# Chunk 4's norm, transposes, Q, K and V worked in a gate-up stage; the first down stage in another order; exponential, value loads and the last down weights issued at other points

## The chip, the core and the metric

One core of a Trainium2 chip. The metric is the device time of one execution in microseconds (us). Engines are called PE (matrix), DVE (vector), ACT (scalar), POOL and SP; here the last two mostly issue transfers. Each engine works through its own instructions strictly in the order in which they stand in the program.

## What is computed

One transformer block with conditioning (adaptive layer norm) over 2048 rows of 576 values, in bfloat16: sliding local attention, then a gated product as feed-forward part.

```
mod = silu(c) @ w_mod  ->  sa, ca, ga, sb, cb, gb          (576 each)
h = layernorm(x) * (1 + ca) + sa
q, k, v = h @ wqkv                                         (32 heads of 18)
logits[s, w] = q[s] . k[s - 2w] * scale, w = 0..7          (8 keys, every second row back)
x = x + ga * (softmax(logits) @ v) @ wo
h = layernorm(x) * (1 + cb) + sb
x = x + gb * ((h @ w_gate) * (h @ w_up)) @ w_down          (576 -> 4608 -> 576)
```

## The kernel before

**Chunks and stages.** The rows are cut into eight chunks of 256 for the attention, and into five groups (line 43) for the feed-forward part: row tiles of 128, (0,2), (2,6), (6,10), (10,13), (13,16). For each group there is a gate-up stage (`gate_up`, line 734: 36 column blocks f of 128) and a down stage (`down`, line 790: the same 36 blocks as depth). They are called G0, D0, G1, D1, up to G4, D4 here. What comes ahead of G0 handles chunk 0 and the projections of chunks 1 and 2.

**Attention beside it.** The attention of the other chunks is cut into pieces, closures in lists with a guessed cost each, and `spread` (line 724) hands them out over the 36 blocks by the sum of costs. A list for gate-up stages is in `gbg` (line 1118), one for down stages in `dbg` (line 1139). Since every engine keeps program order, a piece on PE that waits holds back all the matmuls behind it, those of the feed-forward part too.

**One chunk's way.** `a_ln`, `a_norm` (338, 343): statistics and norm on DVE, with Ln and Exp on ACT (`rsq`, 258) between the two. `a_t` (358): T, ten transposes on PE into `hT`, evicted by DVE (line 286) or ACT (line 288). `a_q` (387): Q and K in five groups (line 377). `a_v` (395): V, written to DRAM (`vd`, line 411). `b_p` (421): eight products prod = q times shifted k on DVE (line 425). `b_lq` (429): twice 20 matmuls that sum them by head (`lg`, 435). `b_lt` (445): transposes of the logits (`lt`). `b_sm0` (454): maximum, difference, Exp on ACT (464). `b_sm1` (467): sums and quotient on DVE. `b_ld` (413): shifted values from DRAM into `vsh`, 1152 KB for each 128 rows, issued by POOL. `b_mul`, `b_add` (481, 487): values times weights, summed on DVE (485, 492, 494, 496) into `o_sb`. `b_o` (498): transposes of `o_sb` (line 505). `b_w` (649): output projection (`pw`, 658) and its eviction on DVE (660, 661). `b_ln`, `b_norm`, `b_t`: second norm and its transposes into `h2T`, which the next gate-up stage reads.

**Pairs.** Depth 576 is four and a half times 128. In the gate-up stages two matmuls of 64 rows each run side by side in the two halves of the array (`half`, line 513). `pair_unit` (526) does the same for Q, K and V of a chunk: units between the blocks of a gate-up stage, nine half steps for a pair of products in place of ten. Before, chunks 5, 6 and 7 (`PAIRED`, line 42) are done so in G1, G2 and G3; chunks 3 and 4 are projected in D0 with five depth steps each, the fifth half empty. `load_pair_rows` (519), the last piece of D0, loads what the pairs need in the upper 64 rows.

**D0 before.** The list is `gb_row` (1132: the row gb, ten matmuls; it also issues load 2 of the down weights, whose buffer it has just read), then chunk 1's output mixed with chunk 3's projections and 14 DVE pieces `b_mul`/`b_add` of chunk 2 (lines 1122 to 1130), then chunk 2's output mixed with chunk 4's norm, T, Q, K and V.

**Loads.** Gate and up weights (`load_wgu`, 145) are issued by SP, one block for four f, three buffers. Down weights (`load_wd`, 160) are issued by POOL, one block of 576 KB for four f, three buffers: block n + 3 is issued when block n has been used. Value loads of chunk 7 (`values(7)`) are issued both at once in G3.

Of the kernel before, what the change touches and what calls it, by code (L numbers as in the profile page):

```python
# [38 lines left out]

MODK = (0, 4, 1, 2, 3)  # L40
QKK = (0, 1, 4, 2, 3)
PAIRED = (5, 6, 7)
GROUPS = [(0, 2), (2, 6), (6, 10), (10, 13), (13, 16)]


# [1 line left out]
def kernel(  # L47
# [84 lines left out]
    def load_x(i):  # L132
        if i < NCH:
            x_in[i] = sp.tile([P, ST, D], BF, name="x_t1") if i == 1 else xin.tile([P, ST, D], BF, name="x_t")
            nc.sync.dma_start(x_in[i][:], x_rows(i))
# [22 lines left out]
            nc.sync.dma_start(wgr[64 * t:64 * (t + 1), cs], wsrc[KF * P:D, cs])  # L158

    def load_wd(g):  # L160
        if g >= NG * NBLK:
            return
        r0 = (g % NBLK) * FB * P
        wb = wdp.tile([P, FB, D], BF, name="wd")
        wd_blk[g] = wb
        return nc.gpsimd.dma_start(wb[:], B_w_down[r0:r0 + FB * P, :].rearrange("(k p) n -> p k n", p=P))  # L166

    def load_k(dst, wsrc, c0, n):
        r = nc.sync.dma_start(dst(slice(0, P), slice(0, KF)), wsrc[0:KF * P, c0:c0 + n].rearrange("(k p) n -> p k n", p=P))
# [168 lines left out]
    def a_ln(i):  # L338
        x = x_in.pop(i)
        xn, rsq, norm = layernorm(lambda j: x[:, j, :], "a")  # L340
        aa[i] = dict(xn=xn, rsq=rsq, norm=norm)

    def a_norm(i):
        aa[i]["rsq"]()
        aa[i]["norm"]()
# [12 lines left out]
    def a_t(i, on_dve=(0, 1, 2), between=None):  # L358
        a_tiles(i)
        hT = aa[i]["hT"]  # L360
        transposed(aa[i]["xn"], lambda m: hT[:, m, :], (0, 1), 0, between, KT if i in PAIRED else KF)(on_dve)

# [24 lines left out]
    def a_q(i, g):  # L387
        qk_tiles(i, QGRP[g], slice(0, CH), nc.scalar.copy)
        if g == 2:
            a_halo(i)  # L390
# [22 lines left out]
    def b_ld(i, j):  # L413
        b = bb.setdefault(i, dict(prod={}, vsh={}))
        base = HALO + i * CH + j * P - DIL * (W - 1)
        vsh = vshp.tile([P, W, DH, H], BF, name="vsh")
        vsrc = bass.AP(vd.tensor, vd.offset + base * D, [[D, P], [DIL * D, W], [1, D]])
        b["vsh"][j] = vsh
        return nc.gpsimd.dma_start(vsh[:].rearrange("p w d h -> p w (d h)"), vsrc)  # L419
# [9 lines left out]
    def b_lq(i, wq):  # L429
        b = bb[i]  # L430
        if wq == 0:
            b["lg"] = ps([P, 2, CH], F32, "lg")
        for m in range(KT):
            for wl in range(4):
                nc.tensor.matmul(b["lg"][H * wl:H * (wl + 1), wq, :], lhsT=ind[:, m, :], rhs=b["prod"][4 * wq + wl][:, m, :],  # L435
                                 start=(m == 0), stop=(m == KT - 1), skip_group_check=True)
        for wl in range(4):
            b["prod"].pop(4 * wq + wl)
        if wq == 1:
            lgs = lgp.tile([P, 2, CH], BF, name="lgs")  # L440
            nc.scalar.copy(lgs[:], b.pop("lg")[:])
            b["lgt"] = lgp.tile([P, 2, ST, 4, H], BF, name="lgt")
            b["lgs"] = lgs

    def b_lt(i):
        b = bb[i]
        lgs = b.pop("lgs")
        pt = ps([P, 2, ST, P], BF, "lt")
        for a in range(2):
            for j in range(ST):  # L450
                nc.tensor.transpose(pt[:, a, j, :], lgs[:, a, js(j)], ident[:])
        nc.scalar.copy(b["lgt"][:].rearrange("p a j w h -> p (a j w h)"), pt[:].rearrange("p a j n -> p (a j n)"))

    def b_sm0(i):
        b = bb[i]
        lg = b.pop("lgt")
        mx = smp.tile([P, ST, 4, H], BF, name="mx", tag="tree")
        dd = smp.tile([P, 2, ST, 4, H], F32, name="dd")
        nc.vector.tensor_tensor(mx[:], lg[:, 0], lg[:, 1], ALU.max)
        nc.vector.tensor_tensor(mx[:, :, 0:2], mx[:, :, 0:2], mx[:, :, 2:4], ALU.max)  # L460
        nc.vector.tensor_tensor(mx[:, :, 0], mx[:, :, 0], mx[:, :, 1], ALU.max)
        for wq in range(2):
            nc.vector.tensor_tensor(dd[:, wq], lg[:, wq], mx[:, :, 0:1].to_broadcast([P, ST, 4, H]), ALU.subtract)
        nc.scalar.activation(dd[:], dd[:], ACTF.Exp, scale=scale)
        b["dd"] = dd

    def b_sm1(i):
        b = bb[i]
        dd = b.pop("dd")
        ss = smp.tile([P, ST, 4, H], F32, name="ss", tag="tree")  # L470
        nc.vector.tensor_tensor(ss[:], dd[:, 0], dd[:, 1], ALU.add)
        nc.vector.tensor_tensor(ss[:, :, 0:2], ss[:, :, 0:2], ss[:, :, 2:4], ALU.add)
        nc.vector.tensor_tensor(ss[:, :, 0], ss[:, :, 0], ss[:, :, 1], ALU.add)
        rs = smp.tile([P, ST, 1, H], F32, name="rs")
        nc.vector.reciprocal(rs[:, :, 0], ss[:, :, 0])
        attn = attnp.tile([P, 2, ST, 4, H], BF, name="attn")
        for wq in range(2):
            nc.vector.tensor_tensor(attn[:, wq], dd[:, wq], rs[:].to_broadcast([P, ST, 4, H]), ALU.mult)
        b["attn"] = attn
# [188 lines left out]
    def b_norm(i):  # L668
        bb[i]["rsq"]()
        bb[i]["norm"]()  # L670
# [12 lines left out]
    def B_pr(i, w0, w1):  # L683
        return [(0.83, lambda w=w: b_p(i, w)) for w in range(w0, w1)]

    def B_lq(i, wq):
        return [(0.0, lambda: b_lq(i, wq))]

    def B_sm(i, turned=None):
        return [(0.5, lambda: b_lt(i))] + ([(1.0, lambda: a_t(turned))] if turned else []) + [ (1.2, lambda: b_sm0(i)), (0.6, nop), (1.8, lambda: b_sm1(i))]  # L690

    def B_wait(us):
        return [(us, nop)]

    def B_two(a, b, av_a, av_b, turned=None):
        return (B_pr(a, 0, 6) + B_lq(a, 0) + B_pr(a, 6, 8) + B_pr(b, 0, 2) + B_lq(a, 1) + B_pr(b, 2, 6) + B_lq(b, 0) + B_sm(a)
                + B_pr(b, 6, 8) + av_a[:4] + B_lq(b, 1) + av_a[4:] + B_sm(b, turned) + av_b)

    def B_one(a, ld, av_a):
        return B_pr(a, 0, 4) + ld + B_pr(a, 4, 6) + B_lq(a, 0) + B_pr(a, 6, 8) + B_wait(1.5) + B_lq(a, 1) + B_wait(4.0) + B_sm(a) + av_a  # L700

    def B_av(i):
        r = []
        for j in range(ST):
            r += [(0.7, lambda j=j, w=w: b_mul(i, j, w)) for w in range(0, W, 2)]
            r += [(0.7, lambda j=j: b_add(i, j, 0)), (0.7, lambda j=j: b_add(i, j, 1)), (1.2, lambda j=j: b_add(i, j, 2))]
            if i in (3, 5):
                r.append((0.0, lambda j=j: b_ld(i + 1, j)))
        return r

    def out_qkv(i, n):
        o = [lambda: b_o(i), lambda: b_w(i, 0), lambda: b_w(i, 1), lambda: b_ln(i), lambda: b_norm(i), lambda: b_t(i, (0,) if i == 6 else (0, 1))]
        if n >= NCH or n == 5 and n in PAIRED:
            return [o[0], nop, o[1], o[2], o[3], o[4], nop, o[5]]
        if n in PAIRED:
            return [lambda: a_ln(n), o[0], lambda: (a_norm(n), load_x(n + 2)), o[1], lambda: a_t(n), o[2], o[3], nop, o[4], nop, nop, o[5]]
        q, v = [lambda g=g: a_q(n, g) for g in range(5)], [lambda j=j: a_v(n, j) for j in range(ST)]
        return ([lambda: a_ln(n), o[0], lambda: (a_norm(n), load_x(n + 2))] + [nop] * (3 if n == 4 else 0) + [o[1], lambda: a_t(n), o[2], o[3]] + q[:1] + [o[4]] + q[1:]
                + [o[5]] + v)

    def nop():
# [390 lines left out]
    def res(i):  # L1112
        return (0.0, lambda: load_res(i))

    def values(i):
        return [(0.0, lambda: [b_ld(i, j) for j in range(ST)])]

    gbg = {0: B_two(1, 2, B_av(1) + [res(2), (0.0, load_wm5), (0.0, lambda: load_wd(0))], []),
           1: values(3) + B_two(3, 4, B_av(3) + [res(3), res(4), (2.4, lambda: a_ln(5)), (1.2, lambda: (a_norm(5), load_x(7)))], B_av(4), 5),
           2: values(5) + B_two(5, 6, B_av(5) + [res(5), res(6)], B_av(6)),  # L1120
           3: B_one(7, values(7), B_av(7)) + [res(7)]}
    av2 = [p for _, p in B_av(2)]
    oq = out_qkv(1, 3)
    first = []
    while oq or av2:
        if oq:
            first.append(oq.pop(0))
        if len(first) > 3:
            first += [p for p in av2[:2]]
            del av2[:2]  # L1130

    def gb_row():
        mod_row(lambda p, k: wm5[p, k, :] if k < KF else wm5r[p, :], gb_bc, sc_bc2)()
# [2 lines left out]
        b_ld(2, 1)  # L1136
        load_wd(2)

    dbg = {0: [gb_row] + first + out_qkv(2, 4) + [load_pair_rows],
           1: out_qkv(3, 5) + out_qkv(4, 6),  # L1140
           2: out_qkv(5, 7) + out_qkv(6, 8),
           3: [nop, lambda: b_t(6, (1,))] + out_qkv(7, 8)}
    units = {1: qkv_units(5, [(29, 0, 1), (30, 1, 2), (31, 2, 3), (32, 3, 4), (33, 4, 5)]),
             2: qkv_units(6, [(0, 0, 1), (1, 1, 2), (2, 2, 3), (3, 3, 4), (4, 4, 5)]),
             3: qkv_units(7, [(0, 0, 3), (1, 3, 4), (2, 4, 5)])}
    for gi in range(NG):
# [37 lines left out]
```

## Time and profile before

| | |
|---|---|
| time, three runs | 559.43, 559.93, 561.68 us (median 559.93) |
| profiled execution | 559.92 us, its span 558.2 us |
| busy: PE, weight loads, DVE, ACT, POOL | 548.4, 323.7, 330.1, 251.3, 63.2 us |
| granted PE clock | 1.00 |
| starts of G0, D0, G1, D1 | 49.62, 89.56, 133.28, 214.57 us |
| starts of G3, G4, D4 | 381.24, 474.03, 526.78 us |

A time-line row gives the start and the length in us, engine, line, operation, output and inputs, the shapes, and how many equal instructions it sums up; square brackets hold the idle time ahead of it and what ended it. Matmuls overlap, so their cost is read from one start to the next, not from their length. In a table of windows each row is a stretch of time: its length, the busy time (and number of instructions) of each engine, the granted clock, the share of the DMA engines in use and GB/s.

### The profile page before, as it was taken

The numbers are of one execution on the slowest core, as the hardware profiler recorded it, in microseconds if no ns is written. First come the engines' busy times: TensorE is split into PE (matmuls) and PEld (weight loads), VectorE is DVE, ScalarE is ACT, GpSimd is POOL, SyncE is SP. The second block draws the span as 40 slices with busy tenths as digits, with TensorE's granted clock in tenths as the row PEclk, the third lists the DMA queues.
The fourth block names the chain that finished last, engine by engine and source line by source line (L and its number), as shares of the span: only waits on it lengthen the run. The fifth ranks groups of instructions, "written<-read, shape, count | busy, mean of one in ns | idle before, by whom it ended". The sixth has DMA issues, their size and how long they took to land.

```text
span 558.2 us, 14633 instructions
## 1 busy us (share of the span) xinstructions
PE 548.4 (98%) x6195; PEld 323.7 (58%) x6195; DVE 330.1 (59%) x796; ACT 251.3 (45%) x592; POOL 63.2 (11%) x98
## 2 busy tenths in 40 slices
PE   8999999999999999999999999999999999999996
PEld 4887796665444465555544445556656555555564
DVE  7888798985777763546468686445527615322202
ACT  2746666344555663212655553114556511565500
POOL 3102101123001001112000000111200022000020
PEclk9999999999999999999999999999999999999999
DMA  8999999645647744336624955444685665565063
GB/s 263 281 272 322 345 296 354 213 151 185 236 142 241 229 143 140 109 105 208 229 80 155 300 172 156 128 125 132 201 266 180 207 180 193 167 210 162 2 177 109
DMA packets 70155, 108.38 MB, mean 194 GB/s; under 512 B 3690, under 2 KB 57850, under 8 KB 70090
## 3 DMA queue, kind: packets, MB, share of 16 engines
q1 hardware_dynamic: 58832, 61.50, 35.9%
q0 software_dynamic: 11168, 45.81, 25.6%
q8 instruction: 48, 0.79, 0.6%
q14 instruction: 17, 0.14, 0.1%
q10 hardware_dynamic: 90, 0.15, 0.1%
HBM read 103.00 MB, written 4.44 MB: 192 GB/s over the span
## 4 chain that ended last, share of the span: by engine, by line
PE 56%; issue 27%; DMA 4%; POOL 2%; DVE 1%; ACT 0%; POOLq 0%; SPq 0%; ACTq 0%
PE pg L513 16%; PE acc L803 13%; PE pu L513 13%; PE pp L513 4%; DMA wd<-in_B_w_down_dram 2%; PE pw L658 2%; PE accr L807 2%; POOL wd L166 2%; PE pq L377 2%; DMA wgu<-in_B_w_up_dram 2%; PE lg L435 1%; PE pv L400 1%; PE tr_pA L299 1%; POOL vsh L419 1%; PE oT_pA L505 0%
## 5 line engine op out<-in xcount | busy, mean ns | idle before, releaser
L513 PE MATMUL pg<-h2T,wgu 64*128 64x512 bf16 (+2 forms) x1440 | 279.7, 333 | 0.0
L513 PE MATMUL pu<-h2T,wgu 64*128 64x512 bf16 (+2 forms) x1440 | 277.9, 333 | 0.7 <-DMA wgu<-in_B_w_up_dram 0.7
L513 PEld LDWEIGHTS <-wgu 64*128 64x128 bf16 x2880 | 141.5, 94 | 105.4 <-DMA wgu<-in_B_w_up_dram 1.1
L761 ACT CAST u_sb<-pu 128x512 bf16<-128x512 f32 (+2 forms) x180 | 90.1, 501 | 132.6 <-PE pg L513 128.9
L803 PE MATMUL acc<-wd,hh 128*128 128x512 bf16 (+1 forms) x588 | 142.7, 370 | 0.5 <-DMA wd<-in_B_w_down_dram 0.4
L767 DVE TENSOR_TENSOR hh<-g_sb,u_sb 128x512 bf16<-128x512 bf16 (+2 forms) x180 | 66.8, 372 | 109.6 <-ACT g_sb L762 108.2
L807 PE MATMUL accr<-wd,hh 128*128 128x64 bf16 x576 | 99.4, 193 | 0.7 <-DMA wd<-in_B_w_down_dram 0.7
L762 ACT CAST g_sb<-pg 128x512 bf16<-128x512 f32 (+2 forms) x180 | 91.4, 508 | 0.0
L803 PEld LDWEIGHTS <-hh 128*128 128x128 bf16 x588 | 55.2, 98 | 59.6 <-issue 1.7
L166 POOL DMA_DIRECT2D wd<-in_B_w_down_dram x45 | 33.9, 753 | 255.5 <-PE accr L807 238.3
L513 PE MATMUL pu<-h2T,wgr 64*128 64x512 bf16 (+2 forms) x180 | 60.3, 335 | 0.3 <-ACT u_sb L761 0.3
L513 PE MATMUL pg<-h2T,wgr 64*128 64x512 bf16 (+2 forms) x180 | 60.3, 335 | 0.2 <-DVE h2T L286 0.2
L807 PEld LDWEIGHTS <-hh 128*128 128x128 bf16 x576 | 51.8, 98 | 3.2 <-issue 1.6
L425 DVE TENSOR_TENSOR prod<-qT,kT 128x1280 bf16<-128x1280 bf16 x56 | 44.7, 819 | 8.5 <-ACT kT L356 4.3
L485 DVE TENSOR_TENSOR vsh<-vsh,attn 128x1152 bf16<-128x1152 bf16 x56 | 40.9, 752 | 0.0
L513 PEld LDWEIGHTS <-wgr 64*128 64x128 bf16 x360 | 18.1, 94 | 16.7 <-issue 4.2
L419 POOL DMA_DIRECT2D vsh<-vd x14 | 12.5, 894 | 111.3 <-DVE o_sb L496 69.9
L660 DVE TENSOR_TENSOR x<-pw,ga_bc 128x512 bf16<-128x512 f32 x14 | 9.6, 689 | 25.7 <-PE pw L658 25.7
L286 DVE TENSOR_SCALAR h2T<-tr_pA,modc 128x256 bf16<-128x256 bf16 (+1 forms) x27 | 8.8, 382 | 26.2 <-PE tr_pA L299 26.2
L259 ACT ACTIVATE ln_rstdb<-ln_mvb,eps 128x2 f32<-128x2 f32 (+1 forms) x9 | 2.7, 296 | 44.0 <-DVE ln_mvb L256 44.0
L288 ACT ACTIVATE h2T<-tr_pB,modc 128x256 bf16<-128x256 bf16 (+1 forms) x16 | 7.7, 533 | 30.2 <-PE tr_pB L299 30.2
L492 DVE TENSOR_TENSOR vsh<-vsh 128x1152 bf16<-128x1152 bf16 x28 | 20.5, 752 | 0.0
(212 smaller groups left out, 523.0 us busy)
## 6 DMA issues: line engine op xcount, KB each, us to landing
wd<-in_B_w_down_dram POOLq DMA_DIRECT2D x45, 576.0 KB, 4.5
wgu<-in_B_w_gate_dram SPq DMA_DIRECT2D x45, 512.0 KB, 4.0
wgu<-in_B_w_up_dram SPq DMA_DIRECT2D x45, 512.0 KB, 5.3
vsh<-vd POOLq DMA_DIRECT2D x14, 1152.0 KB, 9.1
x_r<-in_A_x_dram SPq DMA_DIRECT2D x8, 288.0 KB, 6.6
out_dram<-x SPq DMA_DIRECT2D x15, 144.0 KB, 4.4
x_t<-in_A_x_dram SPq DMA_DIRECT2D x7, 288.0 KB, 6.8
vd<-v_sb POOLq DMA_DIRECT2D x14, 144.0 KB, 3.8
```

Source lines behind the costliest of these rows:

```text
L166: return nc.gpsimd.dma_start(wb[:], B_w_down[r0:r0 + FB * P, :].rearrange("(k p) n -> p k n", p=P))
L377: nc.tensor.matmul(pq[:, gi, :], lhsT=qk_w(kt, m), rhs=hT[:, kt, cols], start=(kt == 0), stop=(kt == KT - 1))
L419: return nc.gpsimd.dma_start(vsh[:].rearrange("p w d h -> p w (d h)"), vsrc)
L425: nc.vector.tensor_tensor(prod[:], aa[i]["qT"][:], aa[i]["kT"][:, :, off:off + CH], ALU.mult)
L485: nc.vector.tensor_tensor(v, v, at, ALU.mult)
L492: nc.vector.tensor_tensor(vsh[:, d], vsh[:, d], vsh[:, 4 + 2 * s:6 + 2 * s], ALU.add)
L513: return nc.tensor.matmul(dst, lhsT=lhs, rhs=rhs, start=first, stop=last, skip_group_check=True)
L761: nc.scalar.copy(u[:, 0:N], pu[:, 0:N])
L762: nc.scalar.copy(g[:, 0:N], pg[:, 0:N])
L767: nc.vector.tensor_tensor(hh[:, f, 0:N], g[:, 0:N], u[:, 0:N], ALU.mult)
L803: nc.tensor.matmul(a[:], lhsT=hh[:, f, js(j)], rhs=wb[:, f % FB, cs], start=(f == 0), stop=(f == FT - 1))
L807: nc.tensor.matmul(accr[:, j, :], lhsT=hh[:, f, js(j)], rhs=wb[:, f % FB, 512:D], start=(f == 0 and j == 0), stop=(f == FT - 1), skip_grou ...
```

## The change

Chunk 4 joins the paired chunks. Its first norm, T and five pair units stand in G1 (units behind blocks 7 to 10), as pieces of a new list `B_mid`, which also norms chunk 5 early and has the transposes of chunks 4 and 5 in one piece with `lg` and `lt`. D0's list is written out anew: chunk 3's projections and chunk 2's output without chunk 4. Exp becomes a piece of its own behind `b_sm0`. `lg` of a second chunk stands behind `lt` of the first in one piece. The two value loads of chunk 7 are issued at two points of G3. The last four blocks of down weights are loaded in G4 into the buffers of `vsh`.

```diff
-PAIRED = (5, 6, 7)
+PAIRED = (4, 5, 6, 7)
...
-        if g >= NG * NBLK:
+        if g >= NG * NBLK - 4:
             return
...
+    def early_wd():
+        for n in (NBLK - 4, NBLK - 2):
+            wb = vshp.tile([P, 2, FB, D], BF, name="vsh")
+            for k in range(2):
+                r0 = (n + k) * FB * P
+                wd_blk[(NG - 1) * NBLK + n + k] = wb[:, k]
+                nc.gpsimd.dma_start(wb[:, k], B_w_down[r0:r0 + FB * P, :].rearrange("(k p) n -> p k n", p=P))
...
+        b["dd"] = dd
+
+    def b_exp(i):
+        dd = bb[i]["dd"]
         nc.scalar.activation(dd[:], dd[:], ACTF.Exp, scale=scale)
-        b["dd"] = dd
...
-    def B_sm(i, turned=None):
-        return [(0.5, lambda: b_lt(i))] + ([(1.0, lambda: a_t(turned))] if turned else []) + [ (1.2, lambda: b_sm0(i)), (0.6, nop), (1.8, lambda: b_sm1(i))]
+    def B_sm(i, beside=None):
+        return [(0.5, lambda: (b_lt(i), beside and beside())),  (1.2, lambda: b_sm0(i)), (0.8, lambda: b_exp(i)), (0.4, nop), (1.8, lambda: b_sm1(i))]
...
-        return (B_pr(a, 0, 6) + B_lq(a, 0) + B_pr(a, 6, 8) + B_pr(b, 0, 2) + B_lq(a, 1) + B_pr(b, 2, 6) + B_lq(b, 0) + B_sm(a)
-                + B_pr(b, 6, 8) + av_a[:4] + B_lq(b, 1) + av_a[4:] + B_sm(b, turned) + av_b)
+        return (B_pr(a, 0, 6) + B_lq(a, 0) + B_pr(a, 6, 8) + B_pr(b, 0, 2) + B_lq(a, 1) + B_pr(b, 2, 6) + B_sm(a, lambda: b_lq(b, 0))
+                + B_pr(b, 6, 8) + av_a[:4] + B_lq(b, 1) + av_a[4:] + B_sm(b, (lambda: a_t(turned)) if turned else None) + av_b)
+
+    def B_ln(n):
+        return [(2.4, lambda: a_ln(n)), (1.2, lambda: (a_norm(n), load_x(n + 2)))]
+
+    def B_mid(a, b, av_a, av_b, turned):
+        return (B_pr(a, 0, 2) + B_ln(b) + B_pr(a, 2, 6) + [(0.5, lambda: (b_lq(a, 0), a_t(b)))] + B_pr(a, 6, 8) + B_lq(a, 1) + B_ln(turned)
+                + B_wait(2.5) + B_pr(b, 0, 6) + B_sm(a, lambda: b_lq(b, 0)) + B_pr(b, 6, 8) + av_a[:4] + B_lq(b, 1) + av_a[4:]
+                + B_sm(b, lambda: a_t(turned)) + av_b)
...
-           1: values(3) + B_two(3, 4, B_av(3) + [res(3), res(4), (2.4, lambda: a_ln(5)), (1.2, lambda: (a_norm(5), load_x(7)))], B_av(4), 5),
+           1: values(3) + B_mid(3, 4, B_av(3) + [res(3), res(4)], B_av(4), 5),
...
-           3: B_one(7, values(7), B_av(7)) + [res(7)]}
+           3: B_one(7, [(0.0, lambda j=j: b_ld(7, j)) for j in range(ST)], B_av(7)) + [res(7)],
+           4: [(1.0, nop), (1.0, early_wd)]}
...
+    first = ([lambda: a_ln(3), lambda: b_o(1), lambda: (a_norm(3), load_x(5)), lambda: b_w(1, 0)] + av2(2) + [lambda: a_t(3, (0,))] + av2(2)
+             + [lambda: b_w(1, 1)] + av2(2) + [lambda: b_ln(1)] + av2(2) + q3[:1] + av2(2) + [lambda: b_norm(1)] + av2(2) + q3[1:2] + av2(2)
+             + [lambda: b_o(2)] + q3[2:3] + [lambda: b_w(2, 0), lambda: b_t(1), lambda: b_w(2, 1)] + q3[3:4] + [lambda: b_ln(2)] + q3[4:]
+             + [lambda: b_norm(2), lambda: a_v(3, 0), lambda: a_v(3, 1), lambda: b_t(2), load_pair_rows])
...
-    dbg = {0: [gb_row] + first + out_qkv(2, 4) + [load_pair_rows],
+    dbg = {0: [gb_row] + first,
...
-    units = {1: qkv_units(5, [(29, 0, 1), (30, 1, 2), (31, 2, 3), (32, 3, 4), (33, 4, 5)]),
+    units = {1: qkv_units(4, [(7, 0, 1), (8, 1, 3), (9, 3, 4), (10, 4, 5)]) | qkv_units(5, [(29, 0, 1), (30, 1, 2), (31, 2, 3), (32, 3, 4), (33, 4, 5)]),
```

`B_one` takes the two parts of its load list at two points (behind product 3 and behind product 7), and `out_qkv` no longer projects chunk 4; `av2(n)` hands out the next n of the 14 DVE pieces of chunk 2.

## The prediction, made before the changed kernel was run

> **What bounds the kernel now.** First the page's busy times, then the table of windows by stage (its last three columns: granted clock, DMA share, GB/s).
>
> ```profile
> PE 548.4 (98%) x6195; PEld 323.7 (58%) x6195; DVE 330.1 (59%) x796; ACT 251.3 (45%) x592; POOL 63.2 (11%) x98
> ```
> ```profile
> 89.56:133.28 43.72, 42.98 (x386) 27.04 (x385) 35.02 (x92) 20.60 (x55) 9.35 (x14) 1.00 0.63 200
> 133.28:214.57 81.29, 81.24 (x874) 39.47 (x873) 58.64 (x122) 46.37 (x93) 5.40 (x7) 1.00 0.60 196
> ```
>
> PE is busy nearly throughout, at full clock (1.00), so PE work removed shortens the run, unless PE must then wait. D0 (first row, 43.72 us) has DVE at 35.02, G1 (second row) has room on DVE and ACT. An average hides where D0's DVE work lies, so the time lines of D0 come next: DVE, then PE and POOL.
>
> ```profile
> 92.90 0.81 DVE L254 BATCH_NORM_STATS2 ln_statsa<-x_t 128x6 f32<-128x288 bf16 x2
> ...
> 95.48 1.19 DVE L264 TENSOR_SCALAR ln_xn<-x_t,ln_mva,ln_rstda 128x576 bf16<-128x576 bf16 x4 [0.60 <-ACT ln_rstda L260]
> ...
> 102.67 1.42 DVE L492 TENSOR_TENSOR vsh<-vsh 128x1152 bf16<-128x1152 bf16 x2
> ...
> 113.04 0.46 DVE L496 TENSOR_TENSOR o_sb<-vsh 128x576 bf16<-128x576 bf16 x1
> 113.42 1.04 DVE L286 TENSOR_SCALAR h2T<-tr_pA,modc 128x256 bf16<-128x256 bf16 x3
> ```
> ```profile
> 99.49 0.19 PE L807 MATMUL accr<-wd,hh 128*128 128x64 bf16 x1
> 100.06 0.38 PE L803 MATMUL acc<-wd,hh 128*128 128x512 bf16 x1 [0.38 <-DMA wd<-in_B_w_down_dram]
> ...
> 114.35 0.61 PE L505 MATMUL oT_pA<-ident,o_sb 128*128 128x128 bf16 x8
> ```
> ```profile
> 92.01 0.76 POOL L166 DMA_DIRECT2D wd<-in_B_w_down_dram  x1 [4.16 <-PE pb L324]
> ```
>
> From 92.90 to 113.42 DVE has one gap, 0.60 us. Its last piece there is chunk 2's `o_sb`, ready at 113.42; PE takes it up at 114.35, 0.9 us later, without a stall, because it had chunk 4's and more of chunk 3's matmuls to do. The second fence shows PE stopped before block 8 until load 2 of the down weights is there; POOL issued it at 92.01, after the gb row, and it took 8.0 us (the view of that tile: issue to landing up to 8.0).
>
> **The change, part by part.** All against the profiled execution, 559.92 us (span 558.2, 1.7 around it, left as it is); the median of three is 559.93, the same.
>
> *Taken out of D0.* Chunk 4's T: 118.09 to 118.65, 0.56. Q and K: four starts-to-next of 1.09 to 1.10 and one of 0.54, 4.93. V: 1.23 and 1.22. Together 7.94 us of PE.
>
> *Put into G1.* Chunk 5's units in G1, the same work, read from the chain of waits:
>
> ```profile
> 195.48 1.09 PE pp L513 x20
> 198.51 1.97 PE pp L513 x36
> 202.42 1.15 PE pp L513 x26
> 205.52 0.83 PE pp L513 x18
> 208.29 1.10 PE pp L513 x18
> 211.34 0.49 PE pp L513 x8
> ```
>
> 6.63 us. T stands behind `lg`: 0.56 and a change of tile shape (four `lt` transposes behind `lg` take 0.33, of which 0.22 are transposes), 0.67. Total 7.3. By PE work alone the move gains 0.6. Both `lg`/`lt` mergers are worth about 0.1 in G0 (0.75 and 0.43 apart, 1.08 together at 151.53) and nothing elsewhere; G0's DVE absorbs it.
>
> *What D0 then waits for.* In the built program's order chunk 2's `o_sb` transposes stand behind down block 21 (before: 20), but only 2 of chunk 3's 5 Q/K groups precede them, and neither V nor any of chunk 4. DVE, however, has the same work ahead of `o_sb` but for two evictions that go to ACT (0.64). A second gate appears: block 8 now stands ahead of `b_w(1,1)`, whose eviction DVE needs. Let load 2 land at L. Then block 8 (0.49) and `pw` (1.22) end at L+1.7; eviction (0.14 of it earlier, the rest 0.72+0.37, and 0.15 to start) at L+2.95; from there to `o_sb` DVE has 10.75 without a gap (102.67 to 113.42). So `o_sb` is ready at L+13.7. I take L = 99.5, 0.5 before today's: Exp stood ahead of gate-up copies on ACT while it waited 1.66 us for DVE (at 88.59), and PE's second `acc` waited 0.25 (89.80 to 90.08) for such a copy; Exp now comes one block later, so the gb row and the load follow sooner. `o_sb`: 113.2. PE, from L+1.7 = 101.2: 13 blocks of 0.49 and two Q/K groups of 1.09 bring it to 109.8, where it waits 3.4 us; ahead of block 8 it waits some 2 us. Behind the transposes it has 14 blocks (6.87), `oT` 0.56, the other Q/K groups 2.73, two `pw` 2.45, two transposes 1.12, V 2.45: 16.2. D0 ends at 129.5 instead of 133.28: **-3.8, not -7.9**. Bounds: with L at 100.5, -2.8; if L never gates, DVE alone (starting at 92.0, 0.9 earlier for the same reason; 7.9 to the eviction, 92.90 to 101.44 less the 0.64; 1.2; 10.75) gives 111.9 and -5.1.
>
> *A new wait in G1.* Chunk 4's norm now lies between chunk 3's products on DVE. Its Exp/Ln stands on ACT behind the third block's copies (140.88 today, 7.6 after G1's start); a norm starts 1.05 after such a copy (183.12, 184.17), so at 8.65, takes 1.1, then a product 0.8, `hh` 0.35, the fourth product 0.75: 11.65. `lg` needs that fourth product and PE is there at 140.29 + 2 blocks of 1.945, 10.9 after the start. Behind `lg` on PE stands all of G1. **+0.8** (0 to 1.4). ACT (46.37 of 81.29) and DVE have room for the rest, PSUM banks asked for were copied out two blocks earlier.
>
> *Loads.* In G3 PE stops at 413.34 and in D4 at 550.49:
>
> ```profile
> 413.34 0.33 PE L513 MATMUL pu<-h2T,wgu 64*128 64x384 bf16 x1 [0.69 <-DMA wgu<-in_B_w_up_dram]
> ```
> ```profile
> 550.49 0.51 PE L807 MATMUL accr<-wd,hh 128*128 128x64 bf16 x12 [0.71 <-DMA wd<-in_B_w_down_dram]
> ```
>
> By starts these are 0.85 and 0.88 us. The first: both value loads (2.3 MB) go out at 398.32 and 399.21 and the DMA share is 0.94 to 1.05 from 400 to 410; the second now goes some 6 us later, when the block's weights are through: **-0.85** (0 to -0.93). The second, and 0.07 to 0.1 just before: the last blocks now go out at block 27 of G4, near 513.6, behind all gate-up loads (last issue 510.6), on POOL with nothing behind them: **-0.95** (-0.7 to -1.0). On SP `load_x(6)` now waits for chunk 4's norm with a gate-up load behind it, some 1.5 us late for a block needed 20 us later: 0.
>
> Sum: -3.8 + 7.3 + 0.8 - 0.85 - 0.95 = **+2.5: 562.4 us**. Low ends give -5.1 + 7.2 - 0.93 - 1.0 = +0.2, high ends -2.8 + 7.4 + 1.4 - 0.7 = +5.3.
>
> **Rivals.** *DVE keeps up in D0.* Then all 7.94 go, and 0.5 of D0's present waits: -7.94 - 0.5 + 7.3 - 1.8 = -2.9, 557.0. For it: PE's 98%; against it: the gapless DVE line above, which no edit shortens by more than a microsecond.
> *Load 2 lands late.* POOL issues the next load once block 3 is done, now about 2 us earlier, into DMA engines that are full until about 102. From the point where L passes 98.5 or so (DVE ready for the eviction at 99.9) each microsecond adds one; L = 102 makes 564.9. Against it: that load was issued later.
> *PE slows after the 3.4 us wait.* The record of clocks shows no change, but the first six `idle` matmuls take 2.74 us (0.42 each), later 512-wide ones 0.21: half rate for some 4 us, 2 us lost. If D0's wait brings that state back: 564.4. The longest pause before, 0.88, did not. The Trainium skill, "TensorE: Matmul & The Clock Gate", section "HAM oscillation — how this bites in real kernels", puts the limit at PE gaps over about 3.4 us; by that rule this wait is just at it; no run here shows it yet.
> *The loads bring nothing*: the waits of G3 and D4 only move: 564.2.
>
> **How the numbers follow.** Forecast 0.62, DVE keeps up 0.14, late load 0.11, slower clock 0.06, loads for nothing 0.07. 0.5% is 2.8 us, about what a measurement here can tell from no change: 557.1 to 562.7. The forecast lies 0.3 inside it; I give 0.40 of its 0.62 to "same" and 0.22 to "slower", and 0.09 of the first rival's 0.14 to "faster". So: faster 0.09, same 0.40 + 0.05 = 0.45, slower 0.22 + 0.11 + 0.06 + 0.07 = 0.46. Range 559.8 to 565.2: the sum's bounds and the three slower rivals; the first rival, 0.14, is left out.
>
> **What would show it.** D0 about 40 us long with PE idle before `oT` of chunk 2, released by DVE `o_sb`, and before block 8, released by the load; G1 about 8 us longer, with a wait of `lg` for a product; no waits at the two loads. It is wrong if D0 ends near 125, or if G1 grows by much more than 8.

## The result, and the profile after

The changed kernel takes 563.83 us (median of 7 runs, 561.23 to 564.6) beside 558.89 for the kernel before (7 runs, 558.59 to 561.68): ratio 1.008, 95% interval 1.0059 to 1.01 (the two medians alone would give 1.009). By the medians it is slower by 4.9 us. The profiled execution took 563.35, with a span of 561.4 against 558.2 before.

The page's first line on PE, and its row of clocks by slices, are these now:

```profile
PE 548.3 (98%) x6256; PEld 323.8 (58%) x6256; DVE 330.1 (59%) x794; ACT 252.4 (45%) x596; POOL 63.1 (11%) x98
...
PEclk9999999899999999999999999999999999999999
```

PE's busy time has not moved (548.4 before), so the 3.2 us of span are idle time of PE; and there is an 8 in the row of clocks, where before the clock was full everywhere. It lies in D0. The table of windows by stage, for D0, G1, G3 and D4 (columns: window, length, busy time of PE, PE weight load, DVE, ACT and POOL, granted clock, DMA share, GB/s):

```profile
88.59:130.34 41.75, 36.26 (x311) 21.21 (x310) 30.40 (x76) 14.68 (x39) 8.16 (x12) 0.96 0.61 192
130.34:219.47 89.13, 88.63 (x1009) 45.79 (x1009) 62.82 (x135) 52.44 (x110) 6.56 (x9) 1.00 0.58 184
386.14:447.50 61.36, 61.36 (x819) 38.02 (x818) 33.68 (x78) 35.99 (x86) 3.67 (x5) 1.00 0.64 203
530.87:557.42 26.55, 26.55 (x253) 17.10 (x252) 3.80 (x11) 0.92 (x3) 1.50 (x2) 1.00 0.17 50
```

D0 lost 7.94 us of PE work and got only 1.97 shorter (43.72 before): PE is idle for 5.5 of its 41.75. G1 grew by 7.84 (81.29 before). G3 and D4 gave back 1.02 and 0.97. The other stages, summed, are 0.8 shorter, above all setup (49.28 against 49.62) and G0 (39.31 against 39.94).

PE's time line in D0 shows both idle spells, the second PE row of each pair being the one that ends the wait:

```profile
96.36 0.19 PE L826 MATMUL accr<-wd,hh 128*128 128x64 bf16 x1
98.85 0.38 PE L822 MATMUL acc<-wd,hh 128*128 128x512 bf16 x1 [2.30 <-DMA wd<-in_B_w_down_dram]
...
99.79 2.32 PE L669 MATMUL pw<-wo,oT 128*128 128x512 bf16 x5
...
114.13 0.56 PE L516 MATMUL oT_pA<-ident,o_sb 128*128 128x128 bf16 x7 [3.12 <-DVE o_sb L507]
...
116.17 1.24 PE L669 MATMUL pw<-wo,oT 128*128 128x512 bf16 x5
```

Ahead of down block 8 PE waits 2.30 for load 2; ahead of chunk 2's `oT` it waits 3.12 for `o_sb`. Between them something else is seen: the same five `pw` matmuls take 2.32 us at 99.79 and 1.24 at 116.17. On DVE's line this is what follows:

```profile
100.01 0.22 DVE L671 TENSOR_TENSOR x<-pwr,ga_bc 128x64 bf16<-128x64 f32 x1 [0.60 <-PE pwr L669]
102.14 0.69 DVE L671 TENSOR_TENSOR x<-pw,ga_bc 128x512 bf16<-128x512 f32 x1 [1.91 <-PE pw L669]
...
113.61 0.46 DVE L507 TENSOR_TENSOR o_sb<-vsh 128x576 bf16<-128x576 bf16 x1
```

DVE stands 2.5 us for block 8 and its `pw`, and from there to the end of `o_sb` (114.07) it has no gap. To see what PE did I cut D0 into pieces of 3.41 us that end where the slow `pw` begin:

```profile
95.76:99.17 3.41, 1.11 (x13) 0.66 (x11) 3.38 (x8) 1.05 (x3) 0.75 (x1) 1.00 1.05 352
99.17:102.57 3.40, 3.40 (x17) 1.43 (x15) 0.90 (x3) 0.88 (x2) 0.00 (x0) 0.50 0.60 210
...
109.40:112.81 3.41, 1.61 (x14) 0.75 (x12) 3.38 (x8) 0.59 (x1) 0.75 (x1) 1.00 0.62 182
112.81:116.22 3.41, 2.09 (x23) 1.57 (x24) 1.22 (x2) 1.47 (x4) 0.00 (x0) 1.00 0.35 141
```

The granted clock is 0.50 from 99.17 to 102.57 and 1.00 on either side. It followed the shorter wait; the longer one, split between the last two rows, was followed by nothing. The list of single runs says the same of the whole: the run of 561.23 has a mean clock of 1.0, 563.34 and 563.35 have 0.996, and the four from 563.83 to 564.6 have 0.993 or 0.994. One stretch of 3.4 us at half clock is worth 0.003 of a mean over 561; the profiled execution loses another 0.001 behind PE's last work (clock 0.50 from 559.96 on). So 0.996 goes with one stretch and 0.993 or 0.994 with two. Where they lie is seen in the profiled execution alone.

### The profile page after: what moved, and what is told of

It reads as the page before. It is cut to its first block, busy times and chain, and to the rows that moved or that the text cites. A ratio compares the mean times of both kernels' runs of the same rounds, so it can differ in the third digit from the quotient of the medians.

```text
span 561.4 us, 14742 instructions
## 1 busy us (share of the span) xinstructions
PE 548.3 (98%) x6256; PEld 323.8 (58%) x6256; DVE 330.1 (59%) x794; ACT 252.4 (45%) x596; POOL 63.1 (11%) x98
## 4 chain that ended last, share of the span: by engine, by line
PE 81%; DVE 3%; DMA 3%; issue 2%; POOL 0%; ACT 0%; SPq 0%; POOLq 0%
PE pg L524 25%; PE pu L524 21%; PE acc L822 20%; PE pp L524 5%; PE accr L826 3%; PE pw L669 3%; DMA wgu<-in_B_w_up_dram 2%; PE lg L443 2%; DMA wd<-in_B_w_down_dram 1%; PE tr_pA L307 1%; PE oT_pA L516 0%; PE pq L385 0%; DVE vsh L503 0%; DVE vsh L496 0%; DVE ln_xn L272 0%
## 5 line engine op out<-in xcount | busy, mean ns | idle before, releaser
L822 PE MATMUL acc<-wd,hh 128*128 128x512 bf16 (+1 forms) x548 | 134.8, 373 | 2.3 <-DMA wd<-in_B_w_down_dram 2.3
L826 PE MATMUL accr<-wd,hh 128*128 128x64 bf16 x528 | 93.7, 193 | 0.0
L166 POOL DMA_DIRECT2D wd<-in_B_w_down_dram x41 | 30.8, 751 | 254.4 <-PE accr L826 236.9
L524 PEld LDWEIGHTS <-wgr 64*128 64x128 bf16 x360 | 19.6, 94 | 16.5 <-issue 4.3
```

What stands on the lines that cost most here:

```text
L524: return nc.tensor.matmul(dst, lhsT=lhs, rhs=rhs, start=first, stop=last, skip_group_check=True)
L822: nc.tensor.matmul(a[:], lhsT=hh[:, f, js(j)], rhs=wb[:, f % FB, cs], start=(f == 0), stop=(f == FT - 1))
L826: nc.tensor.matmul(accr[:, j, :], lhsT=hh[:, f, js(j)], rhs=wb[:, f % FB, 512:D], start=(f == 0 and j == 0), stop=(f == FT - 1), skip_grou ...
```

## The experiments

Theory: the change costs the sum that was predicted, and the waits that it makes in D0 bring a half clock on top in most executions. Rivals: the clock is a bystander, since DVE sets D0; or D0's waits are cheap because something behind them ends last anyway.

**e1_loads: the loads alone.**

```diff
-        if g >= NG * NBLK:
+        if g >= NG * NBLK - 4:
...
-           3: B_one(7, values(7), B_av(7)) + [res(7)]}
+           3: B_one(7, [(0.0, lambda j=j: b_ld(7, j)) for j in range(ST)], B_av(7)) + [res(7)],
+           4: [(1.0, nop), (1.0, early_wd)]}
```

(With `early_wd` and the two places of `B_one`'s list, both as in the change.)

> The kernel before with only its last loads moved: the last four down blocks of the last stage are loaded at the start of the last gate-up stage, chunk 7's second value load goes some blocks later. Order of PE, norms, exponential as before. Theory (these loads end the two waits, at 413.34 and 550.49 in the profile of before): G3 0.9 to 1.0 us and D4 0.9 to 1.0 us shorter, ratio to before 0.9966, about 557.0 beside 558.9. Rival (the waits only move): within 0.3 us of before, with a wait on a weight load elsewhere in G3 or D4.

Measured: 558.66 beside 558.9, ratio 0.9998 (0.9983 to 1.0012). The rival came: the wait moved. D4 is 26.55 against 27.52, as the theory had it, but G3 is 63.35 against 62.38: it got longer by the same amount, with PE waiting for gate and up weights 0.43 and 1.05 us (at 413.08 and 414.46) in place of 0.69. POOL's line in G3 shows why the second value load did not go later:

```profile
398.65 1.80 POOL L427 DMA_DIRECT2D vsh<-vd  x2 [3.40 <-DVE prod L433]
```

V's two stores were issued at 394.1 and 394.7, and took 4.0 us each to land (the view of that tile). POOL issues the loads in its own order, and nothing else stands between them on POOL, so both go out from 398.65 on, one right behind the other, though the program has the second some blocks later; the product on DVE that the profile names as releaser is done at 398.34, ahead of the second landing.

**e2_warm: PE kept busy through both waits.**

```diff
+    def warm(n):
+        w = ps([P, 512], F32, "warm")
+        for _ in range(n):
+            nc.tensor.matmul(w[:], lhsT=wo[:, 0, 0:P], rhs=wqk[:, 0, 0:512], start=True, stop=True, skip_group_check=True)
...
+    first[7] = beside(first[7], 11)
+    first[23] = beside(first[23], 14)
```

(`beside(p, n)` issues piece p and then `warm(n)`: here ahead of down block 8, and one block ahead of chunk 2's `oT`. Nothing reads the bank.)

> The changed kernel with 11 matmuls of 512 columns that nobody reads, put where PE waits ahead of down block 8 in D0, and 14 more ahead of chunk 2's o_sb transposes. No wait is shortened by them, PE is only kept busy. Theory (after the wait of 2.46 us PE ran at half rate for 3.4 us, and 1.1 to 1.4 us of that passed through the eviction to DVE and so to the end; it strikes some executions and spares others): no half-rate pitch in D0, every time near 561.2, median 2 to 2.6 us below the changed kernel's 563.8, ratio to before 1.004. Rival (the clock costs nothing because DVE sets D0 anyway): median stays at 563 to 564.

Measured: 561.55 (561.08 to 562.8, 6 runs), ratio 1.005 (1.0034 to 1.0065), mean clocks 0.999 and 1.0 in all six. D0 in its profile:

```profile
88.58:128.86 40.28, 39.82 (x336) 23.05 (x334) 30.41 (x76) 14.70 (x39) 8.35 (x12) 1.00 0.62 198
```

41.75 became 40.28 and `o_sb` ended at 112.6 instead of 114.07, with nothing taken away and 25 matmuls added. The clock is no bystander: 1.5 us in D0 of the profiled execution, 2.3 in the median. (As a whole that execution, 562.8, is one of the two longest of the six; its G4 takes 53.98, against 52.95 in the changed kernel's profile.)

**e3_qk_first: other PE work put into the longer wait.**

```diff
-             + [lambda: b_o(2)] + q3[2:3] + [lambda: b_w(2, 0), lambda: b_t(1), lambda: b_w(2, 1)] + q3[3:4] + [lambda: b_ln(2)] + q3[4:]
-             + [lambda: b_norm(2), lambda: a_v(3, 0), lambda: a_v(3, 1), lambda: b_t(2), load_pair_rows])
+             + q3[2:3] + [lambda: a_v(3, 0), lambda: b_o(2)] + q3[3:4] + [lambda: b_w(2, 0), lambda: b_t(1), lambda: b_w(2, 1), lambda: b_ln(2)] + q3[4:]
+             + [lambda: b_norm(2), lambda: a_v(3, 1), lambda: b_t(2), load_pair_rows])
```

> The changed kernel with one Q/K group (0.55) and one V group (1.22) of chunk 3 put ahead of chunk 2's o_sb transposes in D0, where PE waits 3.3 us; two blocks (0.98) go along. Theory (the wait is one of order: PE has enough other work): the wait falls to about 0.6, D0 is 2.5 to 2.8 us shorter, 561.0 to 561.3 with the half-rate stretch still there. Rival (what lies behind o_sb is a chain of its own, through oT, two evictions, a norm on DVE and its transposes, as long as PE's work): the wait comes back ahead of chunk 2's norm transposes at D0's end, 563 to 564.

Measured: 559.15 (12 runs), ratio 1.0005 (0.9993 to 1.0016). The wait ahead of `oT` is 0.66, D0 37.90; it is 4.7 below the changed kernel in the median, more than the 2.8 expected. The expectation had left the half clock in, and the clock was below 0.998 in only 2 of 12 runs. The wait was one of order, and nothing behind `o_sb` took its place. The wait ahead of block 8 is still 2.20 here, so it brings half clock by itself in 2 of 12 runs at most.

**e4_bw_early: DVE freed from the load.**

```diff
-    first = ([lambda: a_ln(3), lambda: b_o(1), lambda: (a_norm(3), load_x(5)), lambda: b_w(1, 0)] + av2(2) + [lambda: a_t(3, (0,))] + av2(2)
-             + [lambda: b_w(1, 1)] + av2(2) + [lambda: b_ln(1)] + av2(2) + q3[:1] + av2(2) + [lambda: b_norm(1)] + av2(2) + q3[1:2] + av2(2)
+    first = ([lambda: a_ln(3), lambda: b_o(1), lambda: (a_norm(3), load_x(5)), lambda: b_w(1, 0)] + av2(2) + [lambda: a_t(3, (0,)), lambda: b_w(1, 1)] + av2(2)
+             + av2(2) + [lambda: b_ln(1)] + av2(2) + q3[:1] + av2(2) + [lambda: b_norm(1)] + av2(2) + q3[1:2] + av2(2)
```

> The changed kernel with chunk 1's second output projection put one block earlier in D0, ahead of down block 8 that waits for load 2 of the down weights. Theory (that load also holds up DVE, through this projection's eviction): DVE is free of its gap of 2.5 us, o_sb of chunk 2 is ready at 110.9 instead of 114.1, PE's wait at block 8 falls from 2.46 to about 1.2 and no half-rate stretch follows, D0 2.7 to 3.2 us shorter, 560.6 to 561.0. Rival (DVE's own work alone sets the time of o_sb, the load counts for little): D0 under 1 us shorter, 563.

Measured: 561.92 (6 runs), ratio 1.0055 (1.0039 to 1.0071); D0 40.68 at clock 0.96. `o_sb` came when the theory said, and the wait ahead of block 8 shrank to 1.05, but the gain went elsewhere:

```profile
111.11 0.93 PE L516 MATMUL oT_pA<-ident,o_sb 128*128 128x128 bf16 x7 [3.36 <-DVE o_sb L507]
```

`oT` takes 0.93 instead of 0.56: PE runs at half clock from 111.0 to 114.4, now behind the other wait, where every PE cycle is on the path. That the slow stretch would vanish was wrong. In this profile it stands behind the longer wait, and five of six runs have a clock of 0.995 to 0.997.

**e8_gaps: how long a pause brings half clock?** The kernel before, with pauses made (one run, 673.62 us):

```diff
+    def gap(n):
+        a, b = ps([P, 512], F32, "gapa"), ps([P, 512], F32, "gapb")
+        nc.tensor.matmul(a[:], lhsT=wo[:, 0, 0:P], rhs=wqk[:, 0, 0:512], start=True, stop=True, skip_group_check=True)
+        for _ in range(n):
+            nc.vector.tensor_copy(b[:], a[:])
+        nc.tensor.matmul(a[:], lhsT=wo[:, 0, 0:P], rhs=wqk[:, 0, 0:512], start=True, stop=True, skip_group_check=True)
...
+            if gi >= 3 and k % 3 == 1:
+                gap((3, 2, 4, 3, 5, 3, 4)[k // 3 % 7])
```

> The kernel before with 26 made pauses of PE in the last two gate-up stages: a matmul that nobody reads, two to five VectorE copies of its bank, and a matmul into the same bank that waits for them; pauses of 1.5 to 4 us, 5 us or more apart. Theory (PE is slowed for one stretch of 3.4 us when it was busy for less than about a third of the 3.4 us before, counted in fixed stretches that run on regardless of the program): pauses of 2.3 us and under never slow it, pauses over about 4.5 always, those between in a part of the cases that grows with their length, each slow stretch 3.4 us long and all of them on one grid of 3.4 us. Rival (a pause of more than 3.4 us slows it and a shorter one never does): only the pauses over 3.4 us are followed by half rate.

Measured, in one profile with 26 pauses: of 4 pauses of 1.6 us none was followed by half clock, of 11 of 2.3 us 7 were, of 6 of 3.0 us 3, and of 5 of 3.7 us all. Every slow stretch begins and ends on one grid of 3.41 us over the 250 us in question, and lasts one step of it, except one that lasted two. Cut along that grid, the windows read so (in pairs: a piece with a pause, and the piece behind it):

```profile
427.80:431.22 3.42, 1.13 (x10) 0.40 (x10) 2.37 (x4) 0.00 (x0) 0.00 (x0) 1.00 0.00 0
431.22:434.63 3.41, 3.41 (x30) 1.45 (x30) 0.36 (x1) 1.02 (x3) 0.00 (x0) 0.50 0.00 0
...
591.64:595.05 3.41, 1.67 (x19) 0.84 (x20) 1.62 (x3) 0.50 (x2) 0.00 (x0) 1.00 0.00 0
595.05:598.47 3.42, 3.42 (x41) 1.81 (x38) 0.82 (x3) 2.08 (x5) 0.00 (x0) 1.00 0.33 81
615.54:618.95 3.41, 1.47 (x17) 0.70 (x18) 1.82 (x3) 0.30 (x1) 0.00 (x0) 1.00 0.00 0
618.95:622.36 3.41, 3.41 (x43) 1.91 (x40) 0.72 (x2) 2.21 (x6) 0.00 (x0) 1.00 0.00 0
```

PE was busy for 1.13 us in the first piece, and the next has 0.50; with 1.67 and 1.47 the next has 1.00. All pieces with 1.31 or less were followed by 0.50; between 1.46 and 1.67 three were not and one (1.61) was. So it is the share of a fixed piece that counts, with a border between 38 and 49%, and whether a pause of 2 to 3 us brings half clock depends on where it falls on the grid. D0's own profiles agree: pieces with 0.15 to 1.35 us were followed by half clock (the changed kernel, e4_bw_early, e9_nosplit, e11_load2), pieces with 1.46 to 1.61 were not (the changed kernel, e3_qk_first, e9_nosplit, e11_load2). The theory had a border of a third and pauses of 2.3 us as always safe; both were off. The rival, a limit of 3.4 us on a single pause, is refuted: 10 of the 21 shorter ones were followed by half clock. The Trainium skill, "TensorE: Matmul & The Clock Gate", section "What's actually happening", has a free-running window of 3413 ns, which is the grid seen here; the limit of the section "HAM oscillation — how this bites in real kernels" (PE gaps over some 3.4 us) is not what these runs show.

**e5_exp_loads: loads and the later exponential, without chunk 4's move.** Beside e1_loads:

```diff
-        nc.scalar.activation(dd[:], dd[:], ACTF.Exp, scale=scale)
         b["dd"] = dd
+
+    def b_exp(i):
+        dd = bb[i]["dd"]
+        nc.scalar.activation(dd[:], dd[:], ACTF.Exp, scale=scale)
...
-        return [(0.5, lambda: b_lt(i))] + ([(1.0, lambda: a_t(turned))] if turned else []) + [ (1.2, lambda: b_sm0(i)), (0.6, nop), (1.8, lambda: b_sm1(i))]
+        return [(0.5, lambda: b_lt(i))] + ([(1.0, lambda: a_t(turned))] if turned else []) + [ (1.2, lambda: b_sm0(i)), (0.8, lambda: b_exp(i)), (0.4, nop), (1.8, lambda: b_sm1(i))]
```

> The kernel before with the last loads moved, as in e1_loads, and with the exponential issued one background piece later, as in the changed kernel. Chunk 4 and the first down stage are as before. Theory (it is the later exponential that shortens G0 by 0.63 and that lets chunk 7's values through earlier in G3, both seen in every profile of the changed order and not in e1_loads): G0 39.3, G3 61.4 instead of 63.35, D4 26.55, together 2.6 below before: ratio 0.9955, about 556.3. Rival (G0 and G3 changed for another reason of the new order): G0 39.9 and G3 62.4 to 63.4 as in e1_loads, 558.7.

Measured: 557.84 beside 559.11, ratio 0.9964 (0.9947 to 0.998). G0 is 39.31: the exponential alone takes the 0.63 off. Before, it stood on ACT ahead of the gate-up copies while it waited for DVE, and PE waited for one of these copies:

```profile
68.23 0.63 ACT L464 ACTIVATE dd<-dd 128x512 f32<-128x512 f32 x1 [0.71 <-DVE dd L463]
...
69.17 0.27 PE L513 MATMUL pu<-h2T,wgr 64*128 64x256 bf16 x1 [0.26 <-ACT u_sb L761]
```

G3 is 62.08, with a wait of 0.39 for up weights still there (at 412.39): between the theory's 61.4 and the rival's 62.4, so the later exponential does not explain G3's gain.

**e9_nosplit: the changed kernel, chunk 7's value loads together again.**

```diff
-           3: B_one(7, [(0.0, lambda j=j: b_ld(7, j)) for j in range(ST)], B_av(7)) + [res(7)],
+           3: B_one(7, values(7), B_av(7)) + [res(7)],
```

(And `B_one` as before.)

> The changed kernel with chunk 7's two value loads issued together again, as before; all else as changed. Theory of the prediction (the later second load ends G3's wait): G3 grows from 61.36 to 62.3, with a wait of 0.9 for a weight load. Rival (in the new order the stores of chunk 7's V land 1.3 to 1.9 us sooner and both value loads go ahead of the weights' congestion; the split itself does nothing): G3 stays within 0.1 of 61.36.

Measured: G3 61.36, to 0.01 the same as with the split; 563.02 in one run. The split does nothing. In the changed kernel the loads go out at these times (G3 starts at 386.14, V's stores are issued 12.75 later, in every kernel here):

```profile
398.89 1.11 POOL L592 DMA_DIRECT2D vd<-v_sb  x2 [11.63 <-ACT v_sb L589]
401.56 0.90 POOL L427 DMA_DIRECT2D vsh<-vd  x1 [1.56 <-DMA vd<-v_sb]
403.04 0.91 POOL L427 DMA_DIRECT2D vsh<-vd  x1 [0.58 <-DMA vd<-v_sb]
```

That is 15.4 and 16.9 us into the stage, against 17.1 and 18.0 before, since the stores take 2.1 and 3.0 us to land, not 3.8 and 3.9. It goes with the order of D0 and G1 (2.1 to 3.0 in the eight profiles that have chunk 4 in G1, 3.3 to 4.0 in before, e1_loads and e5_exp_loads); whether that order is the cause, and by what way it would reach a store 250 us later, is not settled. This run shows one more thing: its two waits in D0 are close to those of the changed kernel (2.20 and 3.41 beside 2.30 and 3.12), and this time half clock followed the second and not the first.

**e6_orders: three orders mended.** e3_qk_first and e4_bw_early together, and in G1:

```diff
-        return (B_pr(a, 0, 2) + B_ln(b) + B_pr(a, 2, 6) + [(0.5, lambda: (b_lq(a, 0), a_t(b)))] + B_pr(a, 6, 8) + B_lq(a, 1) + B_ln(turned)
+        return (B_pr(a, 0, 2) + B_ln(b)[:1] + B_pr(a, 2, 4) + B_ln(b)[1:] + B_pr(a, 4, 6) + [(0.5, lambda: (b_lq(a, 0), a_t(b)))] + B_pr(a, 6, 8) + B_lq(a, 1) + B_ln(turned)
```

> The changed kernel with three orders mended: chunk 3's Q/K group and V group ahead of chunk 2's o_sb transposes (as in e3_qk_first), chunk 1's second projection ahead of down block 8 (as in e4_bw_early), and in G1 two of chunk 3's products put between the statistics of chunk 4's norm and the norm itself, into the 1.95 us in which DVE waited for ACT there. Theory: D0 36.3 to 36.9 us with no PE wait over 1.3 us and no half-rate stretch; in G1 the wait of 0.76 us ahead of the first lg is gone, 88.4; together 557.0 to 557.6, ratio 0.997. Rival (the wait for the load is paid anyway once o_sb no longer hides it, and another wait ahead of lg takes the place of the first): D0 37.9, G1 89.1, 559.

Measured: 557.45 (556.8 to 558.53, 12 runs) beside 559.11, ratio 0.9968 (0.995 to 0.9986). D0 36.69, G1 88.53, no wait of `lg`, clocks 0.998 to 1.0. All as expected, and faster than before; the changed kernel had 1.008. It cannot be told from e5_exp_loads (557.84), which leaves chunk 4 in D0. The stages say the same: D0 and G1 together take 125.22 us here, 124.93 in e5_exp_loads and 125.01 in the kernel before. With its waits mended, the move itself is worth nothing.

**e10_loads_order and e11_load2: load 2 ahead of chunk 2's second value load.** e11 is this edit in the changed kernel; e10 is the same in e6_orders, with chunk 3's second V group moved ahead of `oT` as well (and its fourth Q/K group behind chunk 2's projections).

```diff
-        b_ld(2, 1)
         load_wd(2)
+        b_ld(2, 1)
```

> The order of e6_orders, with load 2 of the down weights issued ahead of chunk 2's second value load instead of behind it, and chunk 3's other V group also ahead of chunk 2's o_sb transposes. Theory (load 2 lands late because the value load of 1.2 MB is ahead of it; what PE then waits for is o_sb, and V fills that): wait of 1.2 ahead of block 8 gone, D0 35.5 instead of 36.7, 556.2 to 556.6. Rival (the engines are full until about 98 whatever the order, or the chain behind o_sb ends last): D0 36.5 to 37, no change beside e6_orders.

> The changed kernel with one edit: load 2 of the down weights is issued ahead of chunk 2's second value load. Theory: it lands at 95 to 97 instead of 98.85, the wait ahead of block 8 falls under 0.7 and takes DVE's gap along, o_sb is ready near 111.6; PE is at its transposes by 107 and waits 4 us or more, which fills a stretch of 3.4 us to over 60% in nearly every execution, so that half rate follows there and costs 1.7 behind o_sb: D0 40.3 to 40.9 and 562.0 median, about as e4_bw_early, and lower clocks than 0.998 in nearly every run. Rival (only a pause ahead of block 8 brings half rate): clock 1.0 and 560.3. Rival (load order does nothing): load lands at 98 or later, 563.8.

Measured: e10 558.67, ratio 1.0001 (0.9982 to 1.0019), D0 37.90: worse than e6, and longer than either theory had it. Load 2 is in time now, and load 3 is late instead; and with V gone from behind `o_sb`, the norm there ends last:

```profile
100.37 0.38 PE L822 MATMUL acc<-wd,hh 128*128 128x512 bf16 x1 [1.09 <-DMA wd<-in_B_w_down_dram]
...
122.65 0.34 PE L307 MATMUL tr_pA<-ident,ln_xn 128*128 128x128 bf16 x3 [1.08 <-DVE ln_xn L272]
```

e11: 560.72 (8 runs), ratio 1.0039 (1.0021 to 1.0057), between two of its theories: block 8 no longer waits, load 3 holds PE for 2.15 at block 12, and the wait ahead of `oT` shrinks to 2.07. The clock of its seven other runs is 0.996 to 0.999, below 0.998 in three, where nearly all were expected to be. Its profiled execution, 564.46, had a setup 2.3 us longer than the changed kernel's and is no measure of the edit. But its mean clock of 0.993 stands for two stretches, and only one is in D0 (from 114.39); the other is in the setup:

```profile
8.58:11.99 3.41, 2.09 (x34) 1.36 (x35) 1.81 (x8) 0.66 (x2) 0.45 (x2) 1.00 1.06 316
11.99:15.40 3.41, 3.41 (x35) 3.41 (x34) 2.55 (x9) 0.85 (x3) 1.29 (x5) 0.50 1.08 337
```

PE was busy for 2.09 us (61%) of the piece before, well above the border of e8_gaps. So the busy time in the profile is not the whole rule, and a mean clock does not say in which stage a stretch lies.

## Why the prediction came out as it did

*Sum and range.* 562.4 was forecast, 559.8 to 565.2; 563.83 came. (By its own low ends, +0.2, the range would begin at 560.1.) Without half clock the total holds: the run at clock 1.0 took 561.23, 2.3 above the median of before, and e2_warm lies 2.65 above its own, for +2.5 forecast. In part that is luck: in e2_warm's profile D0 is 0.4 longer than forecast, and G0, forecast at nothing, 0.6 shorter.

*D0, 3.8 less.* Right in mechanism, with both waits at the places named: block 8 some 2 us (2.30), `oT` 3.4 (3.12). Load 2 landed 10.26 into D0 (forecast 9.94). In e2_warm, at full clock, D0 ends 30.1 behind block 8 (forecast 30.0: 129.5 less 99.5), and `o_sb` at L+13.85 (forecast 13.7). In the changed kernel these are 31.5 and 15.2; the difference is the half clock, which delayed `pw`, so its eviction on DVE, so `o_sb`. D0 itself came out at 41.75 instead of 39.9, of which 1.5 are this.

*The step that failed is "PE slows after the 3.4 us wait", held at 0.06.* It was named as a rival and left out of the sum. Six of seven runs have the lower clock, and the mechanism is not as told: half clock followed the wait of 2.30 in the changed kernel's profile and that of 3.41 in e9_nosplit's, and what counts is how little PE does in one piece of the grid, not 3.4 us of idle time on end. The reading "the longest pause before, 0.88, did not" was true and far too short a pause to judge by; between 0.88 and 3.4 no row of the profile said anything, and the limit was taken from a rule in that gap. By their clocks the seven runs have ten such stretches: a run with one took 2.1 more than the run with none (563.35 beside 561.23), one with two some 3. If all ten lie in D0, 10 of 14 waits were followed by one. That is not shown: e11_load2 has one in its setup, and in e3_qk_first the wait ahead of block 8 by itself brought it in 2 of 12 runs at most. The odds of each wait stay open. Both waits should have been given a price, though; that is what the sum missed.

*G1, 8.1 more.* 7.84 came. The wait of the first `lg` was forecast at 0.8. It is 0.50 of idle time and worth 0.60 (G1 is 89.13 here and 88.53 without it, in e6_orders), by the chain that was named: the norm of chunk 4 waits for ACT, and chunk 3's fourth product, the first of the two in the DVE row at 141.16, is done some 11.6 into the stage.

```profile
138.99 1.19 DVE L272 TENSOR_SCALAR ln_xn<-x_t,ln_mva,ln_rstda 128x576 bf16<-128x576 bf16 x4 [1.95 <-ACT ln_rstda L268]
...
141.16 1.55 DVE L433 TENSOR_TENSOR prod<-qT,kT 128x1280 bf16<-128x1280 bf16 x2
...
142.03 0.71 PE L443 MATMUL lg<-prod,ind 128*32 128x256 bf16 x17 [0.50 <-DVE prod L433]
```

The norm starts 8.65 into G1, to the hundredth the forecast. e6_orders put two products into those 1.95 us, and the wait was gone.

*G3, 0.85 less.* 1.02 came, by another cause: the second value load was to go 6 us later, and goes 1.5 behind the first. Undoing the split changes nothing (e9_nosplit), and without chunk 4's move it does not end the wait (G3 63.35 in e1_loads, 62.08 in e5_exp_loads). The loads go sooner because V's stores land sooner, and why they do is open. A right number with a wrong reason, and so luck.

*D4, 0.95 less.* 0.97, and e1_loads shows it by itself.

*G0, nothing.* It gave 0.63. The later exponential was counted for D0 and not for G0, where the same instruction stood ahead of the same copies. The mergers of `lg` and `lt`, which were looked at instead, are worth nothing: e5_exp_loads has none of them and the same 39.31.

*The rivals.* "DVE keeps up" did not happen. Load 2 landed 0.3 later into D0 than assumed, no more. "The loads bring nothing" is half true: the split brings nothing, the early down weights bring 0.97.

## What to carry to other kernels

Moving PE work out of a stage shortens it only as far as the slowest chain through it; look for what each instruction behind the moved work waits for, and fill the time with other work of PE before anything is moved. A PE pause of 2 us or more can cost more than its length: in some executions PE runs at half clock for 3.4 us behind it (7 of the 11 pauses of 2.3 us in e8_gaps), so the spread of single runs and their mean clocks have to be read along with the median. A load that is free to go only when a store has landed goes out with that landing, and a later place in the program does not delay it when its queue has nothing else to issue in between (e1_loads).

## What was not expected of the hardware

In e8_gaps PE's clock changes in fixed pieces of 3.41 us that run on regardless of the program: a piece in which PE was busy for 1.31 us or less was always followed by one at clock 0.50, of four with 1.46 to 1.67 one was, and a busier one was not, as long as the clock was full (15 of 26 pauses brought it). Two cases say that this is not the whole rule: PE was busy for 2.51 us of a slow piece and got a second one (e8_gaps), and 2.09 us of a piece at full clock were followed by a slow one (the setup of e11_load2). The landing time of two stores of 144 KB was 2.1 to 3.0 us or 3.3 to 4.0, along with the order of stages 250 us earlier; why is open.
